# The first block's complex product in 45 frequency steps: two products summed on VectorE and one product of 512 columns back, in place of two products summed in PSUM

## The chip, the core and the metric

The kernel runs on one core of one Trainium2 chip. TensorE multiplies matrices into PSUM, VectorE (DVE), ScalarE (ACT) and GpSimd (POOL) work element by element, SyncE (SP) issues most DMAs. Each engine takes its own instructions strictly in the order of the program; semaphores hold an instruction back until what it needs is there. GpSimd has no access to PSUM. The metric is the device time of one execution in microseconds (us); lower is better.

## What is computed

The reference is a long convolution by FFT, followed by a gated mixture of experts. Only the convolution matters here:

```python
h_filt = (np.maximum(pos_emb @ w1, 0.0) @ w2) * window
u = x * v
L = 2 * S
Uf = np.fft.rfft(u, n=L, axis=1)
Hf = np.fft.rfft(h_filt, n=L, axis=0)
y = np.fft.irfft(Uf * Hf[None, :, :], n=L, axis=1)[:, :S, :]
return (x * y).astype(np.float32)
```

There are 4 sequences of 11456 positions and 128 channels, all in float32. The experts behind it are left out here; the change doesn't touch them.

## The kernel before

The sequence is cut into 3 blocks (NB) of 3840 positions, and the convolution is done by blocks: the spectrum of output block i is the sum over j of input block j times filter block i - j. So block 0 has one complex product, block 1 two, block 2 three. The channels are worked in 4 groups of 32 (NP, DH). A transform of 3840 is split into 60 x 64: a first transform of 60 (the first phase and the function data), one of 64 (spread), the product, one of 64 back, and one of 60 back in the last phase.

The frequency phase (freq_phase) goes through 60 steps: 4 channel groups of 15 steps, each for 4 of the 60 frequencies (KS), worked as two halves of 2 (KH). While it works on groups 0 to 2, it also carries the first transform of the following groups (others: GpSimd's product x * v at L185, the matmuls at L202, ScalarE's copies at L204); in the last 15 steps, the fourth group, it loads and prepares the experts in its place.

On the 128 partitions of a transform of 64, the real parts lie on partitions 0 to 63 and the imaginary parts on 64 to 127. One half step n, j goes like this:

- spread (L366 to L379): TensorE transforms signal and filter together, 480 columns a frequency, into the PSUM tile xp (L373). There is one xp for each half, xp0 and xp1, so the next step's spread waits until VectorE has read this step's. ScalarE then builds from the filter's spectrum the tile g, which holds for each block the filter and the same turned by 90 degrees (the halves of the partitions changed, one with its sign changed: L376, L377, L378).
- combine (L385, L386): VectorE makes the rest of g, from neighbouring filter blocks.
- mult (L393): VectorE multiplies the signal's blocks by g. The block-0 signal gives y (3 blocks x 2 factors, 1536 columns), the block-1 signal p1 (1024 columns), the block-2 signal p2 (512). The factor index a = 0, 1 is the plain and the turned filter: the two terms of a complex product are kept apart.
- After the second half GpSimd adds p1 and p2 into blocks 1 and 2 of y (L465, L466).
- back (L404), one step later (LAG = 1): for each block TensorE takes two products, one with each table c3[:, a], and sums them in PSUM. The tables transform back and form the complex product at once. ScalarE copies the result out (L405), and SyncE stores it.

The order in which a step is written is the order on every engine: half(0), combine(n, 1), back(0) of the step before, the spread of the next step's first half, the carried first transform (step: most times four matmuls of L202 and four copies of L204, in some steps eight, from step 42 on none), store, half(1), back(1), the next step's combine and second spread, GpSimd's sums, back(2). The results of back and of L202 share four PSUM buffers (the pool qps), so each of these products waits until the copy of the fourth one before it is done.

Of the kernel before, what the change touches and what calls it, by code (L numbers as in the profile page):

```python
# [10 lines left out]
F32 = mybir.dt.float32  # L11
# [3 lines left out]
AF = mybir.ActivationFunctionType  # L15
ALU = mybir.AluOpType
# [3 lines left out]
B, S, D = 4, 11456, 128  # L20
E, F = 8, 1024
NB = 3
# [6 lines left out]
DH = D // NP  # L29
# [48 lines left out]
def tables():  # L78

    k1 = np.arange(K1)  # L80
    k2 = np.arange(N2)
    n2 = np.arange(N2)
    n1 = np.arange(K1)
    th = 2 * np.pi * n1[:, None] * (k1[None, :] + 0.25) / K1
    c1 = np.zeros((2, 64, K1, 2))
    c1[:, :K1] = np.stack([np.cos(th), -np.sin(th)], axis=-1)
    ph = 2 * np.pi * n2[None, :, None] * (k1[:, None, None] + 0.25 + K1 * k2[None, None, :]) / L
    c2 = np.zeros((K1, 128, 128))
    c2[:, :64, :64] = np.cos(ph)
    c2[:, 64:, :64] = np.sin(ph)  # L90
    c2[:, :64, 64:] = -np.sin(ph)
    c2[:, 64:, 64:] = np.cos(ph)
    ps = 2 * np.pi * k2[:, None] * n2[None, :] / N2
    c3 = np.zeros((128, 2, 128))
    c3[:64, 0, :64] = np.cos(ps)
    c3[64:, 0, :64] = -np.sin(ps)
    c3[:64, 0, 64:] = np.sin(ps)
    c3[64:, 0, 64:] = np.cos(ps)

    c3 = np.stack([c3[:64, 0], -c3[:64, 0], c3[64:, 0], -c3[64:, 0]]).reshape(2, 128, 128).transpose(1, 0, 2)  # L100
    c3 = np.ascontiguousarray(c3.reshape(128, 2, 2, 64).transpose(0, 1, 3, 2)).reshape(128, 2, 128)
    al = 2 * np.pi * (k1[:, None, None] + 0.25) * (N2 * n1[None, None, :] + n2[None, :, None]) / L
    c4 = np.zeros((128, N2, 64))
    c4[:K1, :, :K1] = np.cos(al) / L
    c4[K1:2 * K1, :, :K1] = -np.sin(al) / L
    pos = np.arange(S, dtype=np.float32)
    win = np.zeros(NB * L, np.float32)
    win[:S] = np.exp(np.float32(-0.01) * pos)
    winp = np.zeros((2, 64, NB, H2), np.float32)
    winp[:, :60] = win.reshape(NB, 60, 2, H2).transpose(2, 1, 0, 3)  # L110
    row = np.arange(128)[:, None] * NS + np.arange(NS) + 1


    e = np.arange(E)
    mine = np.repeat(e, NS)[:, None]
    own, past = (mine == e).astype(float), (mine < e).astype(float)
    sums = np.concatenate([past, own, -(mine == e - 1).astype(float)], axis=1)
    col = np.arange(E * NS)

    shift = np.zeros((E, 2, E))  # L120
    shift[e, 0, e] = -1
    shift[e[1:], 0, e[:-1]] = 1
    shift[-1, 0, -1] = 0
    shift[:, 1] = e[:, None] <= e[None, :]
    bump = np.where(e < E - 1, CAP, 4 * CAP)
    runs = np.concatenate([np.tile(PL * np.arange(PQ), (E, 1)), np.where(e > 0, CAP, 0)[:, None]], axis=1)
    odd = own @ own.T * (col % NS == NS - 1)
    f = np.float32
    return {
        "c1": c1.reshape(128, 2 * K1).astype(f),  # L130
        "c2": np.ascontiguousarray(c2.reshape(K1 // KS, KS, 128, 128).transpose(0, 2, 1, 3)).reshape(K1 // KS, 128, -1).astype(f), "c3": c3.astype(f),
        "c4": np.ascontiguousarray(c4.reshape(128, 2, H2 // C4, C4, 64).transpose(2, 0, 3, 1, 4)).reshape(H2 // C4, 128, -1).astype(f),
        "win": winp.reshape(128, NB * H2), "val": row.astype(np.float16),
        "sums": sums.astype(np.float16), "runs": runs.astype(f), "lines": (PL * np.arange(PQ)).reshape(PQ, 1).astype(f),
        "grid": np.tile(np.arange(PQ + PL, dtype=np.float16) % PQ, (128, 1)),
        "rev": np.tile(np.arange(E, 0, -1, dtype=f), (128, 1)),
        "tri": (np.arange(128)[:, None] <= np.arange(128)[None, :]).astype(np.float16),
        "cols": (col[:, None] < col[None, :]).astype(np.float16), "odd": odd.astype(np.float16),
        "iota": np.tile(np.arange(NTAB, dtype=f), (E, 1)),
        "shift": shift.astype(np.float16), "bump": bump.reshape(E, 1).astype(f),  # L140
    }


class First:
# [6 lines left out]
    ALL = NP * STEPS  # L151
# [155 lines left out]
def freq_phase(tc, nc, i, fi, zd, c3, spare, loads):  # L307
# [6 lines left out]
    PER, KH = K1 // KS, KS // 2  # L314
    ALL = NP * PER
    HERE = spare.shape[1] // 128
    with (
# [48 lines left out]
        def spread(n, j):  # L366

            x1, g = xs[n], gs[n]  # L370
            xp = qpx.tile([128, KH, 512], F32, name=f"xp{j}")
            for k in range(KH):
                nc.tensor.matmul(xp[:, k, 0:(NS + NB) * DH], c2(n % PER * KS + j * KH + k), x1[:, j * KH + k], start=True, stop=True)  # L373
            t = xp[:, :, NS * DH:(NS + NB) * DH].rearrange("p k (s d) -> p k s d", d=DH)
            v = g[:, j].rearrange("p s a k d -> p a k s d")
            nc.scalar.copy(v[0:64, 1], t[64:128])  # L376
            nc.scalar.activation(v[64:128, 1], t[0:64], AF.Copy, scale=-1.0)  # L377
            nc.scalar.copy(v[:, 0, :, 0], t[:, :, 0])  # L378
            xps[n, j] = xp  # L379

        def combine(n, j):
# [3 lines left out]
            nc.vector.tensor_tensor(v[:, 0, :, 1:], t[:, :, 1:], v[:, 1, :, 0:NB - 1], ALU.subtract)  # L385
            nc.vector.tensor_tensor(v[:, 1, :, 1:], t[:, :, 0:NB - 1], v[:, 1, :, 1:], ALU.add)  # L386

        def mult(o, n, j, blk):

            m = 2 * (NB - blk)  # L390
            x = xps[n, j][:, :, blk * B * DH:(blk + 1) * B * DH].rearrange("p k (b d) -> p k b d", d=DH)
            v = gs[n][:, j, 0:NB - blk].rearrange("p s a k d -> p (s a) k d")
            nc.vector.tensor_tensor(o[:, :, :, j * KH:(j + 1) * KH].rearrange("p s a k b d -> p (s a) k b d"),  # L393
                                    x[:, None].broadcast_to([128, m, KH, B, DH]),
                                    v[:, :, :, None, :].broadcast_to([128, m, KH, B, DH]), ALU.mult)

        def backer(n, y):
            h, k = divmod(n, PER)
            z = qp.tile([128, KS, NS, DH], F32, name="z", bufs=4)

            def back(blk):
                zps = qps.tile([128, 512], F32, name="ps").rearrange("p (k b d) -> p k b d", k=KS, b=B)
                for a in range(2):
                    nc.tensor.matmul(zps, c3[:, a, :], y[:, blk, a], start=(a == 0), stop=(a == 1))  # L404
                nc.scalar.copy(z[:, :, blk * B:(blk + 1) * B], zps)  # L405
                if blk == NB - 1:
                    done_z.append((h, k, z))
            return back
# [12 lines left out]
        xs = {n: load(n) for n in range(QX - 1)}  # L421
        for _ in range(LEAD):
            next(todo)
        gs, xps = {}, {}

        def begin(n, j):
            if n < ALL:
                if j == 0:
                    gs[n] = qp.tile([128, 2, NB, 2, KH, DH], F32, name="g")
                spread(n, j)  # L430
        begin(0, 0)
        begin(0, 1)
        combine(0, 0)
        for n in range(ALL + LAG):
            back = backer(n - LAG, ys.pop(n - LAG)) if n >= LAG else lambda blk: None
            if n + QX - 1 < ALL:
                xs[n + QX - 1] = load(n + QX - 1)
            if n >= ALL - PER:
                next(loads, None)

            def half(j):
                mult(y, n, j, 0)
                mult(p1, n, j, 1)
                mult(p2, n, j, 2)
                del xps[n, j]
            if n < ALL:
                y = ys[n] = qp.tile([128, NB, 2, KS, B, DH], F32, name="y", bufs=3)
                p1 = qp.tile([128, NB - 1, 2, KS, B, DH], F32, name="p1")
                p2 = qp.tile([128, 1, 2, KS, B, DH], F32, name="p2")
                half(0)  # L450
                combine(n, 1)
            back(0)
            begin(n + 1, 0)
            step()
            store()
            if n < ALL:
                half(1)
                del gs[n], xs[n]
            back(1)
            if n + 1 < ALL:  # L460
                combine(n + 1, 0)
            begin(n + 1, 1)
            if n < ALL:
                if n < ALL - 1:
                    nc.gpsimd.tensor_tensor(y[:, 1:], y[:, 1:], p1, ALU.add)  # L465
                    nc.gpsimd.tensor_tensor(y[:, 2:], y[:, 2:], p2, ALU.add)  # L466
                else:
                    nc.gpsimd.tensor_tensor(y[:, 1], y[:, 1], p1[:, 0], ALU.add)
                    nc.vector.tensor_tensor(y[:, 2], y[:, 2], p1[:, 1], ALU.add)
                    nc.vector.tensor_tensor(y[:, 2], y[:, 2], p2[:, 0], ALU.add)  # L470
            back(2)
# [801 lines left out]
def program(tc, i, out):  # L1273
    nc = tc.nc
# [4 lines left out]
    with tc.tile_pool(name="mc", bufs=1) as mc:  # L1279
        wf = mc.tile([128, 2 * E * F], F32, name="wf")  # L1280
        fi = First(nc, i, x1d, x1f, mc, wf)
        spare = wf[:, fi.used:]
        c3 = mc.tile([128, 2, 128], F32, name="c3")
        first_phase(tc, fi)
        nc.scalar.dma_start(c3, i["c3"])
        nc.scalar.dma_start(zd.rearrange("p h r w -> (p h) r w")[:, H2 * 2 * K1:], i["none"])
# [73 lines left out]
```

## Time and profile before

| what | value |
|---|---|
| time, median of 3 runs | 1626.85 us (1624.58 to 1632.59) |
| the profiled execution's own time | 1626.78 us |
| its span, from first to last instruction | 1625.0 us |
| L404, the products back, on TensorE | 720 records of 597 ns, 331.3 us |
| L393, the complex products, on VectorE | 240 + 120 records, 217.4 + 210.8 us |
| L465, L466, GpSimd's sums | 59 of 4537 ns and 59 of 2356 ns |
| share of TensorE in the chain that ended last | 84% |

A float32 matmul shows as two records in the trace, each with a weight load (PEld) beside it, so the 360 products of L404 are 720 records. Rows of instructions in order of time give the start in us from the span's start, the length in us, engine, line, operation, output<-inputs, and the number of merged instructions; in brackets stands how long the engine was idle before, and what ended that. Rows of groups give the count, then busy time in us, mean length in ns, and the idle time before. Rows of stretches give the limits, the length, the busy time of PE, PEld, DVE, ACT and POOL each with its number of instructions, the granted TensorE clock, the busy share of the DMA engines and GB/s. A row of one line over the whole run gives the least, median and greatest length in ns. Ends of matmuls are modelled, and neighbouring rows of one engine can overlap.

### The profile page before, as it was taken

The numbers are of one execution on the slowest core, as the hardware profiler recorded it, in microseconds if no ns is written. First come the engines' busy times: TensorE is split into PE (matmuls) and PEld (weight loads), VectorE is DVE, ScalarE is ACT, GpSimd is POOL, SyncE is SP. The second block draws the span as 40 slices with busy tenths as digits, with TensorE's granted clock in tenths as the row PEclk, the third lists the DMA queues.
The fourth block names the chain that finished last, engine by engine and source line by source line (L and its number), as shares of the span: only waits on it lengthen the run. The fifth ranks groups of instructions, "written<-read, shape, count | busy, mean of one in ns | idle before, by whom it ended". The sixth has DMA issues, their size and how long they took to land.

```text
span 1625.0 us, 26505 instructions
## 1 busy us (share of the span) xinstructions
PE 1537.8 (95%) x8272; PEld 961.0 (59%) x8272; DVE 1203.4 (74%) x2424; ACT 794.3 (49%) x1677; POOL 1084.8 (67%) x850
## 2 busy tenths in 40 slices
PE   7985999999999999996789999999989999999997
PEld 2552444444444444442347766666767888888997
DVE  1324877888788799993877777777887777777886
ACT  4552455444544544442235544544345655556774
POOL 1112988888888878870156647855677888867885
PEclk9996999999999999997889999999999999999999
DMA  7998999999999799968978768877631111111110
GB/s 283 333 339 315 379 377 377 356 329 335 321 343 338 255 265 316 312 160 295 301 222 255 229 214 257 255 223 240 209 87 33 47 45 47 45 37 37 38 36 23
DMA packets 198532, 361.92 MB, mean 223 GB/s; under 512 B 64650, under 2 KB 138778, under 8 KB 198350
## 3 DMA queue, kind: packets, MB, share of 16 engines
q1 hardware_dynamic: 181078, 320.12, 58.9%
q0 software_dynamic: 16704, 38.89, 8.5%
q8 instruction: 67, 1.10, 0.3%
q10 hardware_dynamic: 608, 1.20, 0.2%
q14 instruction: 75, 0.61, 0.1%
HBM read 216.96 MB, written 145.69 MB: 223 GB/s over the span
## 4 chain that ended last, share of the span: by engine, by line
PE 84%; DMA 6%; DVE 5%; issue 3%; POOL 1%; ACT 1%; SPq 0%; DVEq 0%; ACTq 0%; POOLq 0%
PE ps L404 20%; PE xp L373 12%; PE bank L782 6%; PE y L1018 5%; PE ps L202 5%; PE my L834 4%; PE my L832 4%; PE hp L700 4%; PE my L833 4%; PE hp L702 4%; PE hp L701 4%; PE mh L700 2%; PE tp L1031 2%; PE mh L702 1%; PE mh L701 1%
## 5 line engine op out<-in xcount | busy, mean ns | idle before, releaser
L404 PE MATMUL ps<-y,c 128*128 128x512 f32 x720 | 331.3, 597 | 0.3
L465 POOL TENSOR_TENSOR y<-y,p 128x2048 f32<-128x2048 f32 x59 | 267.7, 4537 | 68.8 <-DVE p L393 68.8
L706 POOL DMA_INDIRECT out<-o,ids x186 | 199.9, 1075 | 123.3 <-DVE o L713 87.0
L404 PEld LDWEIGHTS ps<-y,c 128*128 128x128 f32 x720 | 133.4, 190 | 173.0 <-issue 155.9
L637 POOL DMA_INDIRECT xt<-out,ids x186 | 193.1, 1038 | 49.3 <-issue 30.6
L393 DVE TENSOR_TENSOR p<-xp,g 128x1024 f32<-128x1024 f32 x240 | 217.4, 947 | 0.0
L393 DVE TENSOR_TENSOR y<-xp,g 128x1536 f32<-128x1536 f32 x120 | 210.8, 1757 | 4.1
L821 DVE SCALAR_TENSOR_TENSOR hh<-hp,hh 128x1024 fp32r<-128x1024 f32 x130 | 158.4, 1219 | 68.3 <-ACT hh L820 68.1
L405 ACT COPY z<-ps 128x512 f32<-128x512 f32 x180 | 105.6, 586 | 176.5 <-PE ps L404 167.5
L820 ACT ACTIVATE hh<-hp 128x1024 fp32r<-128x1024 f32 x130 | 134.2, 1032 | 75.4 <-PE hp L702 75.4
L589 POOL DMA_INDIRECT lists<-pl,lies x32 | 53.6, 1676 | 141.0 <-DVE step L1116 72.3
L466 POOL TENSOR_TENSOR y<-y,p 128x1024 f32<-128x1024 f32 x59 | 139.0, 2356 | 4.6
L677 DVE TENSOR_TENSOR ws<-wf,ws 128x1024 fp32r<-128x1024 f32 x104 | 126.7, 1219 | 15.5 <-ACT ws L672 12.1
L610 POOL MEMSET idle<- 128x512 f16 x248 | 134.6, 543 | 0.2
L1018 PE MATMUL y<-zt,c 128*64 128x512 f32 x384 | 114.1, 653 | 19.8 <-DMA zt<-zd 11.2
L700 PE MATMUL hp<-hl,ws 128*128 128x512 f32 (+1 forms) x344 | 123.3, 359 | 3.5 <-DVE tb L626 1.9
L202 PE MATMUL ps<-wf,c 60*120 60x384 f32 x512 | 111.8, 532 | 14.8 <-DVE wf L185 14.3
L782 PEld LDWEIGHTS bank<-wd,h 128*128 128x128 f32 x896 | 104.2, 191 | 31.5 <-issue 31.4
L373 PE MATMUL xp<-x,wf 128*128 128x480 f32 x256 | 115.5, 575 | 7.3 <-issue 3.6
L204 ACT COPY wf<-ps 120x384 f32<-120x384 f32 x256 | 105.5, 493 | 29.5 <-PE ps L202 28.9
L702 PE MATMUL hp<-hl,ws 128*128 128x512 f32 (+1 forms) x344 | 116.4, 338 | 0.0
L834 PE MATMUL my<-hh,ws 128*128 128x512 f32 (+1 forms) x344 | 116.3, 338 | 0.0
(162 smaller groups left out, 3062.1 us busy)
## 6 DMA issues: line engine op xcount, KB each, us to landing
wf<-xv SPq DMA_DIRECT2D x64, 768.0 KB
zt<-zd SPq DMA_DIRECT2D x64, 768.0 KB
x1d<-wf SPq DMA_DIRECT2D x64, 720.0 KB
x<-x1d SPq DMA_DIRECT2D x60, 768.0 KB
zd<-z SPq DMA_DIRECT2D x118, 384.0 KB
out<-xm SPq DMA_DIRECT2D x96, 258.0 KB
ox<-xo SPq DMA_DIRECT2D x96, 256.0 KB
x1f<-fx POOLq DMA_DIRECT2D x16, 720.0 KB
```

Source lines behind the costliest of these rows:

```text
L202: nc.tensor.matmul(ps[p], self.c1[rows], u[rows, q * RUN:(q + 1) * RUN], start=True, stop=True)
L373: nc.tensor.matmul(xp[:, k, 0:(NS + NB) * DH], c2(n % PER * KS + j * KH + k), x1[:, j * KH + k], start=True, stop=True)
L393: nc.vector.tensor_tensor(o[:, :, :, j * KH:(j + 1) * KH].rearrange("p s a k b d -> p (s a) k b d"), x[:, None].broadcast_to([128, m, KH, ...
L404: nc.tensor.matmul(zps, c3[:, a, :], y[:, blk, a], start=(a == 0), stop=(a == 1))
L465: nc.gpsimd.tensor_tensor(y[:, 1:], y[:, 1:], p1, ALU.add)
L637: ins = nc.gpsimd.indirect_dma_start(out=xt[:, j], out_offset=None, in_=self.rows[0:have], in_offset=bass.IndirectOffsetOnAxis(ap=ids[:, j ...
L700: nc.tensor.matmul(hp, w[:, 0, c], hl[:, 0], start=True, stop=False)
L702: nc.tensor.matmul(hp, w[:, 1, c], hl[:, 0], start=False, stop=True)
L706: ins = nc.gpsimd.indirect_dma_start(out=self.rows, out_offset=bass.IndirectOffsetOnAxis(ap=ids[:, j:j + 1], axis=0), in_=o, in_offset=Non ...
L782: nc.tensor.matmul(bank[:, j * D:(j + 1) * D], h[f][:, j * 128:(j + 1) * 128], wd[s][:, f * D:(f + 1) * D], start=(f == 0), stop=(f == F / ...
L834: nc.tensor.matmul(y, w2[:, 1, c], h[:, 0], start=False, stop=(f == F // 128 - 1))
L1018: nc.tensor.matmul(y[p * 64:(p + 1) * 64], c4s[ch // C4][:, ch % C4, p, :], z[:, NP * p:NP * (p + 1)], start=True, stop=True)
```

## The change

In steps 0 to 44 (whole(n): all but the last channel group) block 0 is treated in another way. ScalarE makes, besides g, two more tiles for each half step: w, which holds the real part of the filter's first block on both halves of the partitions and then its imaginary part on both halves (four copies of 64 partitions x 64 columns), and turn, the block-0 signal turned by 90 degrees (two instructions of 64 partitions x 256 columns). The mult of the block-0 signal then leaves block 0 of the output out (low = 1: four factors in place of six). A new function, first, multiplies the signal by the one part of w and turn by the other, and sums the two products: three VectorE instructions of 256 columns, the last two with all their inputs in SBUF. The sum overwrites the first product in y. The way back of block 0 is then one product of 512 columns with a third table c3[:, 2], which transforms back and nothing else. Blocks 1 and 2, and all of the last 15 steps, are as before.

```diff
+    c3 = np.concatenate([c3, np.concatenate([c3[:64, 0], c3[:64, 1]])[:, None]], axis=1)
...
+            if whole(n):
+                turns[n, j] = qp.tile([128, KH, B * DH], F32, name=f"turn{j}", bufs=1)
             xp = qpx.tile([128, KH, 512], F32, name=f"xp{j}")
...
             nc.scalar.copy(v[:, 0, :, 0], t[:, :, 0])
+            if whole(n):
+                w, turned = ws[n][:, j], turns[n, j]
+                for half in range(2):
+                    here, there = slice(half * 64, half * 64 + 64), slice(64 - half * 64, 128 - half * 64)
+                    for a in range(2):
+                        nc.scalar.copy(w[here, a], t[a * 64:a * 64 + 64, :, 0])
+                    nc.scalar.activation(turned[here], xp[there, :, 0:B * DH], AF.Copy, scale=2.0 * half - 1.0)
             xps[n, j] = xp
...
-        def mult(o, n, j, blk):
-
-            m = 2 * (NB - blk)
+        def whole(n):
+            return n < ALL - PER
+
+        def first(y, n, j):
+
+            ks = slice(j * KH, (j + 1) * KH)
+            shape = [128, KH, B, DH]
+            x = xps[n, j][:, :, 0:B * DH].rearrange("p k (b d) -> p k b d", d=DH)
+            for a, v in enumerate((x, turns.pop((n, j)).rearrange("p k (b d) -> p k b d", d=DH))):
+                nc.vector.tensor_tensor(y[:, 0, a, ks], v, ws[n][:, j, a][:, :, None, :].broadcast_to(shape), ALU.mult)
+            nc.vector.tensor_tensor(y[:, 0, 0, ks], y[:, 0, 0, ks], y[:, 0, 1, ks], ALU.add)
+
+        def mult(o, n, j, blk, low=0):
+
+            m = 2 * (NB - blk - low)
...
-            v = gs[n][:, j, 0:NB - blk].rearrange("p s a k d -> p (s a) k d")
+            v = gs[n][:, j, low:NB - blk].rearrange("p s a k d -> p (s a) k d")
...
-                for a in range(2):
-                    nc.tensor.matmul(zps, c3[:, a, :], y[:, blk, a], start=(a == 0), stop=(a == 1))
+                if blk == 0 and whole(n):
+                    nc.tensor.matmul(zps, c3[:, 2, :], y[:, 0, 0], start=True, stop=True)
+                else:
+                    for a in range(2):
+                        nc.tensor.matmul(zps, c3[:, a, :], y[:, blk, a], start=(a == 0), stop=(a == 1))
...
             def half(j):
-                mult(y, n, j, 0)
+                mult(y[:, 1:] if whole(n) else y, n, j, 0, int(whole(n)))
                 mult(p1, n, j, 1)
                 mult(p2, n, j, 2)
+                if whole(n):
+                    first(y, n, j)
                 del xps[n, j]
...
-        c3 = mc.tile([128, 2, 128], F32, name="c3")
+        c3 = mc.tile([128, 3, 128], F32, name="c3")
```

How this stands on the engines is shown at two places of step 15. On VectorE, before, the second half of step 15 and the combine of the next step (xp is the half's PSUM tile, p the tiles p1 and p2; the numbers are those of the buffers):

```order
L393 TENSOR_TENSOR y<-xp_1849,g 128x6x256
L393 TENSOR_TENSOR p_1866<-xp_1849,g 128x4x256
L393 TENSOR_TENSOR p_1867<-xp_1849,g 128x2x256
L385 TENSOR_TENSOR g<-xp_1878,g 128x2x2x32
L386 TENSOR_TENSOR g<-xp_1878,g 128x2x2x32
```

The same place on VectorE in the changed kernel, whose lines are numbered anew (L415 is mult, L407 and L408 are first, L395 and L396 combine):

```order
L415 TENSOR_TENSOR y<-xp_2159,g 128x4x256
L415 TENSOR_TENSOR p_2182<-xp_2159,g 128x4x256
L415 TENSOR_TENSOR p_2183<-xp_2159,g 128x2x256
L407 TENSOR_TENSOR y<-xp_2159,w 128x256
L407 TENSOR_TENSOR y<-turn_2158,w 128x256
L408 TENSOR_TENSOR y<-y 128x256
L395 TENSOR_TENSOR g<-xp_2198,g 128x2x2x32
L396 TENSOR_TENSOR g<-xp_2198,g 128x2x2x32
```

The first mult has lost two of its six factors, and three instructions stand between the last mult and the next combine; two of them read no PSUM tile.

On ScalarE, before, from the spread of step 15's first half to that of its second (z is the output of back, wf the buffer of the carried transform):

```order
L376 COPY g<-xp_1817 64x2x3x32
L377 ACTIVATE g<-xp_1817 64x2x3x32
L378 COPY g<-xp_1817 128x64
L204 COPY wf<-ps 120x384 x4
L405 COPY z<-ps 128x4x128
L376 COPY g<-xp_1849 64x2x3x32
```

The same stretch of ScalarE in the changed kernel (L379 to L381 make g, L387 makes w, L388 makes turn, L205 is the copy of the carried transform, L430 that of z):

```order
L379 COPY g<-xp_2117 64x2x3x32
L380 ACTIVATE g<-xp_2117 64x2x3x32
L381 COPY g<-xp_2117 128x64
L387 COPY w<-xp_2117 64x64 x2
L388 ACTIVATE turn_2116<-xp_2117 64x256
L387 COPY w<-xp_2117 64x64 x2
L388 ACTIVATE turn_2116<-xp_2117 64x256
L205 COPY wf<-ps 120x384 x4
L430 COPY z<-ps 128x4x128
L379 COPY g<-xp_2159 64x2x3x32
```

Six instructions now stand between the copies that make g and those of the carried transform. GpSimd's instructions and their order are the same in both kernels.

More of the change, by code (lines that the diff above doesn't have):

```diff
@@ L423, in freq_phase @@
             next(todo)
-        gs, xps = {}, {}
+        gs, xps, ws, turns = {}, {}, {}, {}
         def begin(n, j):
@@ L429, in begin @@
                     gs[n] = qp.tile([128, 2, NB, 2, KH, DH], F32, name="g")
+                    if whole(n):
+                        ws[n] = qp.tile([128, 2, 2, KH, DH], F32, name="w")
                 spread(n, j)
@@ L441, in half @@
             def half(j):
-                mult(y, n, j, 0)
+                mult(y[:, 1:] if whole(n) else y, n, j, 0, int(whole(n)))
                 mult(p1, n, j, 1)
                 mult(p2, n, j, 2)
+                if whole(n):
+                    first(y, n, j)
                 del xps[n, j]
```

## The prediction

> **What bounds the kernel now.** I read the head of the page first, then two stretches of the trace, then single instructions in order of time.
>
> ```profile
> span 1625.0 us, 26505 instructions
> PE 1537.8 (95%) x8272; PEld 961.0 (59%) x8272; DVE 1203.4 (74%) x2424; ACT 794.3 (49%) x1677; POOL 1084.8 (67%) x850
> 148.00:600.00 452.00, 447.08 (x1242) 195.51 (x1242) 365.58 (x452) 222.24 (x580) 384.26 (x134) 1.00 0.96 337
> 294.90:305.00 10.10, 10.09 (x29) 4.38 (x28) 8.14 (x11) 5.00 (x13) 8.68 (x3) 1.00 1.04 371
> ```
>
> The profiled execution took 1626.78 us, 1.8 more than its span, and the median is 1626.85, so no correction is needed. The third row is the stretch of the first 45 steps, the fourth one step of it; after the length stand the busy times of PE, PEld, DVE, ACT and POOL, then the granted clock. In a step of 10.10 us TensorE is busy throughout, at full clock; GpSimd has 1.42 us free, VectorE 1.96 and ScalarE 5.10. A product taken from TensorE would pay at once, if nothing else grows past 10.10 us. The limits of the whole stretch are its two ends:
>
> ```profile
> 147.99 1.76 DVE L393 TENSOR_TENSOR y<-xp,g 128x1536 f32<-128x1536 f32 x1
> 600.32 1.74 DVE L393 TENSOR_TENSOR y<-xp,g 128x1536 f32<-128x1536 f32 x1
> ```
>
> VectorE begins step 0 at 147.99 and step 45 at 600.32: 45 steps in 452.3 us.
>
> **What is removed: TensorE.**
>
> ```profile
> 576.41 3.60 PE L404 MATMUL ps<-y,c 128*128 128x512 f32 x8
> 579.84 0.57 PE L373 MATMUL xp<-x,c 128*128 128x480 f32 x1
> ```
>
> Eight records of L404 take 579.84 - 576.41 = 3.43 us, 0.43 each, and one product is two records. Each of 45 steps loses one product, 0.86 us. If TensorE stayed the bound that would be 45 x 0.86 = 39 us.
>
> **What is added: VectorE's own time.** Per half step the block mult writes 1024 columns in place of 1536, and three instructions of 256 columns are new.
>
> ```profile
> 292.57 0.29 DVE L385 TENSOR_TENSOR g<-xp,g 128x128 f32<-128x128 f32 x1 [0.88 <-ACT g L378]
> 292.90 0.29 DVE L386 TENSOR_TENSOR g<-xp,g 128x128 f32<-128x128 f32 x1
> 293.23 1.76 DVE L393 TENSOR_TENSOR y<-xp,g 128x1536 f32<-128x1536 f32 x1
> 294.90 1.81 DVE L393 TENSOR_TENSOR p<-xp,g 128x1024 f32<-128x1024 f32 x2
> ...
> L393 DVE TENSOR_TENSOR p<-xp,g 128x1024 f32<-128x1024 f32 x90 | 109.3, 1214 | 0.0
> L393 DVE TENSOR_TENSOR p<-xp,g 128x512 f32<-128x512 f32 x90 | 61.3, 681 | 0.0
> ```
>
> I count from start to start, since neighbours overlap: 1.214 + 0.681 - 1.81 = 0.085 us. The two combines take 293.23 - 292.57 = 0.66. A mult of 1024 columns takes 1.214 - 0.085 = 1.13, one of 512 0.60. For 256 columns I go between 0.29 (128) and 0.681 (512): 0.42. The first new mult overlaps its successor (0.335); the second, and the sum, end before what follows may start (L385 to L386: 0.33 for 0.29), so 0.455 each. A half step is 0.66 + 1.13 + 1.13 + 0.60 + 0.335 + 0.455 + 0.455 = 4.77, a step 9.53 us. So without any wait VectorE would still be under 10.10.
>
> **What is added: VectorE and GpSimd collide.** This is the term that decides. Everything VectorE does now in these steps has one operand in PSUM (xp). The new second mult (turn times w) and the sum (y plus y) have both inputs in SBUF. Before has one place where VectorE does that while GpSimd adds:
>
> ```profile
> 724.25 2.35 POOL L468 TENSOR_TENSOR y<-y,p 128x1024 f32<-128x1024 f32 x1 [1.40 <-DVE p L393]
> ...
> 724.62 3.06 DVE L469 TENSOR_TENSOR y<-y,p 128x1024 f32<-128x1024 f32 x1
> 727.71 1.23 DVE L470 TENSOR_TENSOR y<-y,p 128x1024 f32<-128x1024 f32 x1
> ```
>
> L469 and L470 are the same sum. L470, with GpSimd idle, takes 1.23 us; L469, begun 0.37 after GpSimd's L468, takes 3.06 and ends 727.68 - 726.60 = 1.08 us after GpSimd does: it stood still until GpSimd had finished. GpSimd itself was not slowed (2.35 us here, 2.35 for L466 below). The counterweight is L677, also SBUF with SBUF, beside GpSimd's indirect DMAs and memsets:
>
> ```profile
> L677 DVE TENSOR_TENSOR ws<-wf,ws x104: 1202/1216/1227, 828.4 to 1610.3; 128x1024 fp32r<-128x1024 f32 x104
> ```
>
> None of 104 is stretched, so it takes a GpSimd instruction that reads SBUF as L468 does. In the Trainium skill, the page "SBUF — State Buffer", section "Who interferes with whom", states just this: a VectorE instruction with two SBUF inputs contends with a GpSimd instruction that reads SBUF, and whoever is second waits for the whole of the first. It speaks against this change. By it the two waits below are full ones; were the port shared in slices they would be near nothing. L469 shows a full wait, once.
>
> GpSimd's work in a step:
>
> ```profile
> 286.10 4.55 POOL L465 TENSOR_TENSOR y<-y,p 128x2048 f32<-128x2048 f32 x1 [1.36 <-DVE p L393]
> 290.72 2.35 POOL L466 TENSOR_TENSOR y<-y,p 128x1024 f32<-128x1024 f32 x1
> 293.03 1.82 POOL L185 TENSOR_TENSOR wf<-wf 124x768 f32<-124x768 f32 x1
> 296.19 4.54 POOL L465 TENSOR_TENSOR y<-y,p 128x2048 f32<-128x2048 f32 x1 [1.34 <-DVE p L393]
> ```
>
> L465 begins as soon as the second half's first p is written (294.90 + 1.214 = 296.11; L465 at 296.19). Put 0 at the end of that p. GpSimd holds 0.08 to 4.62. VectorE does the other p and the first new mult, and reaches the second at 1.13 + 0.60 + 0.335 - 1.214 = 0.85. As with L469 (1.08 after the release, 0.15 less than alone) it ends at 4.62 + 0.42 - 0.15 = 4.89 in place of 0.85 + 0.42 = 1.27: **3.62 us lost**. L466 follows L465 after 290.72 - 290.65 = 0.07 us, so it is waiting when that mult ends, while the sum can only start 0.03 later: L466 goes first, 4.89 + 2.35 = 7.24, and the sum ends 0.27 after, at 7.51, in place of 4.89 + 0.035 + 0.42 = 5.34: **2.17 us lost**. Then L185 runs to about 9.4. The first half of the next step comes to its second mult at 7.51 + 0.035 + 0.66 + 2.26 + 0.60 + 0.335 = 11.4, when GpSimd is idle, so it loses nothing. The step becomes 9.53 + 3.62 + 2.17 = **15.32 us**, VectorE the bound.
>
> The size of the second wait is unknown. At the low end the sum slips in ahead of L466 and loses nothing: 13.15 us. At the high end L185 too goes first, another 1.82: 17.14. I take the middle, since L466 is queued right behind L465 and VectorE's sum is not ready when the port comes free.
>
> **What is added: ScalarE.** Each half step gains four copies of 64 columns and two turns of 256.
>
> ```profile
> 296.76 0.32 ACT L376 COPY g<-xp 64x192 f32<-64x192 f32 x1 [1.07 <-DVE p L393]
> 297.08 0.32 ACT L377 ACTIVATE g<-xp 64x192 f32<-64x192 f32 x1
> 297.42 0.21 ACT L378 COPY g<-xp 128x64 f32<-128x64 f32 x1
> 297.54 1.63 ACT L204 COPY wf<-ps 120x384 f32<-120x384 f32 x4
> ...
> L405 ACT COPY z<-ps 128x512 f32<-128x512 f32 x130 | 76.2, 586 | 129.1 <-PE ps L404 121.2 <-DMA wf<-xv 6.8 <-DMA zd<-z 1.1
> L204 ACT COPY wf<-ps 120x384 f32<-120x384 f32 x180 | 72.8, 493 | 0.5 <-ACT g L378 0.5
> ```
>
> A copy of 64 columns is 0.21 us (L378). 256 columns lie between 192 (0.32) and 512 (0.586): 0.37. L376 and L377 are followed with no overlap, L378 is followed after 0.12. Wholly without overlap the six add 4 x 0.225 + 2 x 0.38 = 1.66, all overlapped like L378 4 x 0.12 + 2 x 0.28 = 1.04. I take 1.56: five of the six change the half of the partitions that they read or write, as L376 and L377 do. ScalarE goes from 5.00 to 8.1 us a step; with a step of 15.32 that is covered, and the turned values are ready long before VectorE asks for them. Only the first step pays openly, two half steps of copies before VectorE begins: 3 us.
>
> If the cover were gone, it would cost in one place. Four L204 free the PSUM buffers for which the next L404 waits:
>
> ```profile
> 296.61 1.55 PE L202 MATMUL ps<-wf,c 60*120 60x384 f32 x8
> 298.17 1.95 PE L404 MATMUL ps<-y,c 128*128 128x512 f32 x4
> ```
>
> The first L204 ends at 297.54 + 0.49 = 298.03, and L404 starts at 298.17, right after it: TensorE and ScalarE are even here today. So 1.56 us more ahead of L204 moves this product by 1.56, against 0.86 saved: +0.70 a step. The extra c3 columns and SBUF tiles move no transfer that the steps wait for.
>
> **The sum.** 45 x 15.32 = 689.4; less 452.3 = 237; with the 3 us at the start 1626.8 + 240 = **1867 us**. Behind step 45 the work is as before and moves as a whole. With the ends of the second wait: 45 x 13.15 gives 1769, 45 x 17.14 gives 1949.
>
> **The rivals.**
> First, no wait between VectorE and GpSimd for such short instructions. For it: L677 never waits, and a 256-column read needs the port for a quarter of a microsecond. Against it: L469. Then ScalarE's copies decide, 45 x 0.70 = 32 and 3 at the start: 1661 us.
> Second, on the other side, **the product saved is really saved**: no port wait, and the new copies overlap or are hidden so that the L404 behind the four L204 is moved by clearly less than 0.86 us. Then TensorE stays the bound and gets 39 us back: 1588. Against it: even the cheapest sum, 1.04, is over 0.86, and TensorE has no slack at that point. If the two about cancel there is no change, within 0.5% or 8 us, about what a measurement of this kernel can tell.
> Third, TensorE loses its clock. In the forecast it works 10.10 - 0.86 = 9.24 us of 15.32 and idles 6 a step, and this trace has a half clock behind shorter gaps:
>
> ```profile
> 793.71 0.16 PE L548 MATMUL bank<-tnt,shift 8*8 8x1 f16 x1 [1.93 <-DVE tnt L542]
> ...
> 795.00:799.00 4.00, 4.00 (x24) 1.74 (x22) 3.63 (x14) 1.04 (x3) 0.00 (x0) 0.57 0.66 179
> ```
>
> A 1.93 us gap, then 0.57 of the clock. The 9.24 us at half clock are 18.5, more than 15.32; held there all the time it would bound the step: 45 x 18.5 gives about 2010. But a busy TensorE has the full clock in this trace, so at most a part of each step is slow, and 6 us of slack cover that.
> In the Trainium skill, "TensorE: Matmul & The Clock Gate", Part 1, puts the idle time that halves the clock at about 3.4 us; this trace has it behind 1.93 us, so the row counts.
>
> **Chances and range.** Forecast with its two ends 0.82, no wait 0.07, lost clock 0.04, real saving 0.04, no change 0.03. So slower 0.93, same 0.03, faster 0.04. The range is the forecast's own, 1769 to 1949, a little widened: 1760 to 1950.
>
> **What would show it.** The new second mult (L407 of the changed kernel, from turn) would have two durations, 0.42 in the first half and about 4 us in the second; the sum (L408) 0.42 and about 2.6. GpSimd's adds stay 4.54 and 2.35. TensorE's busy share in this stretch falls to about 60%, the step is 15.3 us, and the chain of waits runs over VectorE. If L407 and L408 stay near 0.4 us throughout, the port term is wrong, and a step of 10.8 us with TensorE waiting for the copy behind ScalarE's turns would be the first rival. A step of 9.2 to 9.5 us would be the second.

## The result, and the profile after

The changed kernel takes 1853.82 us (median of six runs, 1851.22 to 1855.28) against 1629.45 us for the kernel before (six runs, 1624.58 to 1639.52): a ratio of 1.1358, interval 1.1335 to 1.1381. The forecast was 1867 us.

First the head of the page of the changed kernel, with its row of the granted clock, then the stretch of the first 45 steps and one step in it (columns as in the prediction: length, busy time of PE, PEld, DVE, ACT, POOL, granted clock).

```profile
span 1853.5 us, 27220 instructions
PE 1574.3 (85%) x8182; PEld 956.1 (52%) x8182; DVE 1500.3 (81%) x2694; ACT 920.9 (50%) x2217; POOL 1101.1 (59%) x850
PEclk9977998999999998889989799999999999999999
```

```profile
150.16:822.41 672.25, 484.51 (x1162) 192.35 (x1162) 662.35 (x723) 348.28 (x1117) 399.63 (x137) 0.91 0.74 230
382.56:397.48 14.92, 10.75 (x34) 4.30 (x32) 14.71 (x17) 9.33 (x33) 8.89 (x4) 1.00 0.70 196
```

VectorE is busy 14.71 of 14.92 us in a step, where it had been busy 8.14 of 10.10; TensorE, busy for 10.09 of 10.10 before, now stands still for 4.2. The stretch from VectorE's step 0 to its step 45 has grown from 452.3 to 672.25 us, by 219.9. That leaves 8.6 of the 228.5 us between the two spans: 2.2 at the start (150.16 against 147.99) and 6.4 behind step 45 (1853.5 - 822.41 = 1031.1 against 1024.7), no more than runs of one kernel differ by.

Where the VectorE time sits shows in the same page's groups (busy us, mean ns of one), and in the durations of single source lines (least/median/greatest ns). All 90 instances of a line have one shape, so a mean hides nothing but time:

```profile
L407 DVE TENSOR_TENSOR y<-turn,w 128x256 f32<-128x256 f32 x90 | 198.4, 2204 | 0.0
L408 DVE TENSOR_TENSOR y<-y 128x256 f32<-128x256 f32 x90 | 131.0, 1456 | 3.1
```

```profile
L407 DVE TENSOR_TENSOR y<-xp,w x90: 412/415/416, 153.0 to 814.6; 128x256 f32<-128x256 f32 x90
L407 DVE TENSOR_TENSOR y<-turn,w x90: 415/2288/4098, 153.4 to 815.0; 128x256 f32<-128x256 f32 x90
L408 DVE TENSOR_TENSOR y<-y x90: 424/2177/2466, 155.3 to 819.1; 128x256 f32<-128x256 f32 x90
```

The first mult, which reads xp in PSUM, takes 0.41 us every time. The second, of the same size but from turn in SBUF, goes from 0.415 to 4.1 us, and the sum from 0.42 to 2.47. The timeline of VectorE and of GpSimd over the second half of one step and the first half of the next (start, duration) shows beside what they stretch:

```profile
396.18 1.81 DVE L415 TENSOR_TENSOR p<-xp,g 128x1024 f32<-128x1024 f32 x2
397.91 0.41 DVE L407 TENSOR_TENSOR y<-xp,w 128x256 f32<-128x256 f32 x1
398.24 4.04 DVE L407 TENSOR_TENSOR y<-turn,w 128x256 f32<-128x256 f32 x1
402.31 2.45 DVE L408 TENSOR_TENSOR y<-y 128x256 f32<-128x256 f32 x1
404.69 0.28 DVE L395 TENSOR_TENSOR g<-xp,g 128x128 f32<-128x128 f32 x1
...
408.53 0.41 DVE L407 TENSOR_TENSOR y<-turn,w 128x256 f32<-128x256 f32 x1
408.98 0.43 DVE L408 TENSOR_TENSOR y<-y 128x256 f32<-128x256 f32 x1
```

```profile
397.48 4.52 POOL L494 TENSOR_TENSOR y<-y,p 128x2048 f32<-128x2048 f32 x1 [5.96 <-DVE p L415]
402.07 2.40 POOL L495 TENSOR_TENSOR y<-y,p 128x1024 f32<-128x1024 f32 x1
404.44 1.99 POOL L186 TENSOR_TENSOR wf<-wf 124x768 f32<-124x768 f32 x1
```

GpSimd's first sum ends at 402.00, VectorE's second mult at 402.28; GpSimd's second sum ends at 404.47, VectorE's sum at 404.76. In the first half, at 408.53, GpSimd is idle and the same two instructions take 0.41 and 0.43. The chain of waits, by engine and then by line, ends the reading:

```profile
PE 50%; DVE 32%; issue 9%; DMA 5%; ACT 2%; POOL 0%; SPq 0%; DVEq 0%; ACTq 0%; POOLq 0%
DVE y L407 11%; DVE p L415 8%; DVE y L415 5%; PE ps L429 5%; PE bank L811 4%; PE y L1047 4%; PE xp L376 4%; PE hp L729 3%; PE hp L731 3%; PE my L863 3%; PE my L861 3%; PE my L862 3%; PE hp L730 3%; PE mh L729 2%; PE tp L1060 2%
```

L407 leads it. GpSimd has 0%, although the experiments below show that it is what L407 waits for: L407 has no idle time and no releaser, so the page books the wait as VectorE's own work. Only the spread of durations gives it away. In what follows "the port" stands for whatever the two engines share here; the runs show when one of them waits, not the port itself.

### The profile page after: what moved, and what is told of

It reads as the page before. It is cut to its first block, busy times and chain, and to the rows that moved or that the text cites. A ratio compares the mean times of both kernels' runs of the same rounds, so it can differ in the third digit from the quotient of the medians.

```text
span 1853.5 us, 27220 instructions
## 1 busy us (share of the span) xinstructions
PE 1574.3 (85%) x8182; PEld 956.1 (52%) x8182; DVE 1500.3 (81%) x2694; ACT 920.9 (50%) x2217; POOL 1101.1 (59%) x850
## 4 chain that ended last, share of the span: by engine, by line
PE 50%; DVE 32%; issue 9%; DMA 5%; ACT 2%; POOL 0%; SPq 0%; DVEq 0%; ACTq 0%; POOLq 0%
DVE y L407 11%; DVE p L415 8%; DVE y L415 5%; PE ps L429 5%; PE bank L811 4%; PE y L1047 4%; PE xp L376 4%; PE hp L729 3%; PE hp L731 3%; PE my L863 3%; PE my L861 3%; PE my L862 3%; PE hp L730 3%; PE mh L729 2%; PE tp L1060 2%
## 5 line engine op out<-in xcount | busy, mean ns | idle before, releaser
L429 PE MATMUL ps<-y,c 128*128 128x512 f32 x540 | 255.3, 601 | 43.0 <-ACT wf L205 43.0
L735 POOL DMA_INDIRECT out<-o,ids x186 | 201.6, 1084 | 122.3 <-DVE o L742 86.0
L415 DVE TENSOR_TENSOR p<-xp,g 128x1024 f32<-128x1024 f32 x240 | 217.4, 948 | 0.0
L407 DVE TENSOR_TENSOR y<-turn,w 128x256 f32<-128x256 f32 x90 | 198.4, 2204 | 0.0
L376 PE MATMUL xp<-x,wf 128*128 128x480 f32 x256 | 138.7, 673 | 70.1 <-issue 64.3
L429 PEld LDWEIGHTS ps<-y,c 128*128 128x128 f32 x540 | 100.3, 192 | 177.8 <-issue 171.2
L379 ACT COPY g<-xp 64x192 f32<-64x192 f32 x120 | 37.9, 316 | 282.3 <-PE xp L376 282.2
L415 DVE TENSOR_TENSOR y<-xp,g 128x1024 f32<-128x1024 f32 (+1 forms) x120 | 162.8, 1357 | 4.1
L430 ACT COPY z<-ps 128x512 f32<-128x512 f32 x180 | 103.5, 587 | 117.2 <-PE ps L429 87.1
L376 PE MATMUL xp<-x,c 128*128 128x480 f32 x224 | 118.7, 659 | 47.9 <-issue 46.3
L203 PE MATMUL ps<-wf,c 60*120 60x384 f32 x512 | 125.8, 592 | 18.1 <-DVE wf L186 15.2
L706 DVE TENSOR_TENSOR ws<-wf,ws 128x1024 fp32r<-128x1024 f32 x104 | 127.2, 1223 | 14.0 <-ACT ws L701 10.8
L408 DVE TENSOR_TENSOR y<-y 128x256 f32<-128x256 f32 x90 | 131.0, 1456 | 3.1
L729 PE MATMUL hp<-hl,ws 128*128 128x512 f32 (+1 forms) x344 | 123.5, 359 | 4.5 <-DVE hh L850 2.1
```

The lines of the kernel that those rows point to most:

```text
L407: nc.vector.tensor_tensor(y[:, 0, a, ks], v, ws[n][:, j, a][:, :, None, :].broadcast_to(shape), ALU.mult)
L729: nc.tensor.matmul(hp, w[:, 0, c], hl[:, 0], start=True, stop=False)
L735: ins = nc.gpsimd.indirect_dma_start(out=self.rows, out_offset=bass.IndirectOffsetOnAxis(ap=ids[:, j:j + 1], axis=0), in_=o, in_offset=Non ...
```

## The experiments

Three explanations of the 220 us were set against each other: the port (theory A: VectorE's instructions with two SBUF inputs wait for GpSimd's), ScalarE's six copies in front of L205 (theory B), and new VectorE instructions that are simply slow (theory C). All runs are compared by the stretch from VectorE's step 0 to step 45 (452.3 us before, 672.3 after) as well as by the whole time. A stretch is that of the one profiled execution, and a step is counted from the start of VectorE's first mult to that of the next step's.

**GpSimd's two sums left out in the 45 steps.**

```
@@ the end of the second half step
+                if whole(n):
+                    pass
-                if n < ALL - 1:
+                elif n < ALL - 1:
                     nc.gpsimd.tensor_tensor(...)
```

> The changed kernel without GpSimd's two sums in steps 0 to 44 (blocks 1 and 2 of these steps lack what p1 and p2 bring). Theory A (port: VectorE's instructions with two SBUF inputs stand until GpSimd's sum has ended, 3.6 + 2.0 us a step): the second mult and the sum both take 0.42 us in all 90 half steps, and what limits next is ScalarE's six copies ahead of the carried transform's copies: step 10.8 us, 1661 us (1645 to 1670). Theory B (the new ScalarE copies hold up VectorE): unchanged, step 14.9 us, about 1850. Theory C (these SBUF instructions are slow by themselves): unchanged, about 1850, the second mult still 2.2 us in the mean.

Measured: 1666.4 us, ratio 1.0229 (1.017 to 1.0288); stretch 488.0, a steady step 10.67. Of the 220 us, 184 go with the two sums. The time is the expected one, but the second mult is not at 0.42 us in every half step. The timeline of VectorE in this kernel has the pair of one half step at its own speed, and the mult of the next half step still stretched; GpSimd's timeline names the instruction beside it.

```profile
403.67 0.41 DVE L407 TENSOR_TENSOR y<-turn,w 128x256 f32<-128x256 f32 x1
404.11 0.42 DVE L408 TENSOR_TENSOR y<-y 128x256 f32<-128x256 f32 x1
...
408.40 1.71 DVE L407 TENSOR_TENSOR y<-turn,w 128x256 f32<-128x256 f32 x1
```

```profile
408.03 1.81 POOL L186 TENSOR_TENSOR wf<-wf 124x768 f32<-124x768 f32 x1 [8.87 <-PE ps L203]
```

The instructions aren't slow by themselves. And GpSimd's third SBUF reader, the carried product L186, now falls on VectorE's second mult: it ends at 409.84, the mult at 410.11. In the same step TensorE stands still for 1.41 us until the first L205, behind ScalarE's new copies, is done (TensorE's timeline):

```profile
409.26 1.98 PE L429 MATMUL ps<-y,c 128*128 128x512 f32 x4 [1.41 <-ACT wf L205]
```

**ScalarE's new copies left out after step 0.** The w and turn tiles of step 0 stay in use, and the copies run under `if n == 0`.

> The changed kernel with w and turn made by ScalarE in step 0 alone and read again in all later steps (block 0 is wrong there). Theory A: ScalarE's copies were hidden behind VectorE's waits, so the time stays within 8 us of the changed kernel's 1854 (step 14.9 us). Theory B: the step falls to the 9.5 us of VectorE or the 9.3 us of TensorE, below 1630. Theory C: unchanged, 1854.

Measured: 1874.36 us, ratio 1.1506 (1.1439 to 1.1573); stretch 671.2, step 14.91. The stretch is that of the changed kernel, 672.3: the copies cost nothing while the port is the bound. The whole time is 20 us longer, outside the expected 8. Of these, 18 lie behind step 45 (1049.6 against 1031.1 us), probably because the experts' work there depends on the computed values (the trace has 188 indirect DMAs of line L735 in place of 186); from here on, kernels that compute other values are read by their stretch.

**Both left out.**

> Both left out: no GpSimd sums in steps 0 to 44, and w and turn made in step 0 alone. Theory A: only VectorE's own instructions are left as a bound, 9.53 us a step, 45 x 9.53 = 429 in place of 452: about 1604 us (1595 to 1615), faster than before the change. Theory C: over 1800. Theory B: as its run without copies.

Measured: 1630.64 us, ratio 1.0018 (0.9994 to 1.0042); stretch 447.8. The expectation, 1595 to 1615, was missed. The step is 9.27 us in most of steps 1 to 12 and 10.00 in most from step 14 to 38, where VectorE's timeline shows both instructions stretched again, by L186:

```profile
404.82 1.15 DVE L407 TENSOR_TENSOR y<-turn,w 128x256 f32<-128x256 f32 x1
406.01 1.91 DVE L408 TENSOR_TENSOR y<-y 128x256 f32<-128x256 f32 x1
```

```profile
403.88 3.76 POOL L186 TENSOR_TENSOR wf<-wf 124x768 f32<-124x768 f32 x2 [8.19 <-PE ps L203]
```

Two L186 fill 403.88 to 407.64; the mult ends at 405.97, between them, and the sum at 407.92, after the second. Leaving out two of GpSimd's three readers does not free the port. The 9.27 us of the early steps are VectorE's own time: there L407 and L408 take 0.41 and 0.42 us.

**The sums left out and the copies moved behind L205.** The w and turn copies go into a function of their own, called after the step's L205.

```
+        def extra(n, j):
...
             step()
+            extra(n + 1, 0)
```

> As the run without GpSimd's sums, but ScalarE makes w and turn behind the carried transform's copies and not ahead of them. If it is their place ahead of these copies that makes a step of 10.8 us (TensorE waits for a PSUM buffer), the step falls to 9.5 to 10.1 us, 1605 to 1630. If it is ScalarE's or VectorE's amount of work, it stays as in the run without sums, about 1661.

Measured: 1639.92 us, ratio 1.0056 (1.0036 to 1.0076); stretch 460.0, step 10.11, at the upper end of what was expected; the time is 10 us above it. Against the first experiment (10.67) only ScalarE's order differs, and it is worth 0.56 us a step: a cost that does not show while GpSimd's sums are there. VectorE's second mult still waits for L186, for 0.85 us a step where it was 1.30 in the first experiment, so part of the 0.56 can lie there; the two were not separated.

**The suspected cost by itself, in the kernel before.** One added VectorE instruction of 256 columns per step behind the second half's last p, its result unused: once with both inputs in SBUF, once with one of them in PSUM.

```
+ nc.vector.tensor_tensor(probe, y[:, 0, 0, ks], y[:, 0, 1, ks], ALU.add)      # first kernel
+ nc.vector.tensor_tensor(probe, <xp, block 0>, y[:, 0, 1, ks], ALU.add)       # second kernel
```

> The kernel before, with one VectorE instruction more in steps 0 to 44: behind the second half's last mult a sum of 256 columns with both inputs in SBUF, into a tile that nobody reads. Nothing else of the change. Theory A: it comes 0.5 us after GpSimd has begun its 4.54 us sum and ends with it, some 4.4 us long; VectorE's step becomes 8.12 + 0.42 + 3.95 = 12.5 us, 45 x 12.5 = 562 in place of 452: about 1737 us (1720 to 1750). Without a port wait (or with GpSimd slowed instead) it takes 0.42 us, hidden in VectorE's 1.96 us of slack: 1627.

> The same as the run before it, but one of the two inputs of the added sum is in PSUM (the signal's block 0 in xp). Theory A: no port is shared, 0.42 us, hidden in the slack: within 8 us of 1627. If any instruction more at this place costs, whatever it reads (VectorE is the hidden bound there): the same as the run before it.

Measured: 1718.31 us, ratio 1.0528 (1.0498 to 1.0559), stretch 536.9, step 12.37; and 1633.57 us, ratio 1.0025 (1.0003 to 1.0047), stretch 454.0, step 10.10. The second is as expected. The first is 2 us below its range of 1720 to 1750: the step is nearly the expected one, but in nine of the 45 the probe takes only 0.42 to 1.7 us. The two timelines, first the kernel with SBUF and SBUF, VectorE and GpSimd, then the other:

```profile
402.97 4.36 DVE L448 TENSOR_TENSOR probe<-y 128x256 f32<-128x256 f32 x1
```

```profile
402.53 4.51 POOL L469 TENSOR_TENSOR y<-y,p 128x2048 f32<-128x2048 f32 x1 [3.58 <-DVE p L393]
```

```profile
407.02 0.42 DVE L448 TENSOR_TENSOR probe<-xp,y 128x256 f32<-128x256 f32 x1
```

```profile
406.58 4.54 POOL L469 TENSOR_TENSOR y<-y,p 128x2048 f32<-128x2048 f32 x1 [1.34 <-DVE p L393]
```

Same place, same size, both 0.44 us behind the start of GpSimd's sum: 4.36 us against 0.42. One operand in PSUM is all the difference, and it is 85 us of the stretch against 2. Both read the tile y that GpSimd is adding to, so it is not the tile that one waits for.

**GpSimd kept as busy, but only writing.** Three memsets of 2048 columns (5.53 us) stand in place of the two sums.

```
+                if whole(n):
+                    for _ in range(3):
+                        nc.gpsimd.memset(p1, 0.0)
```

> The changed kernel with GpSimd's two sums of steps 0 to 44 replaced by three memsets of p1, which write SBUF and read nothing (blocks 1 and 2 of these steps lack p1 and p2). If the wait comes from GpSimd reading SBUF: the second mult and the sum stay at 0.42 us beside the memsets, step 10.7 us as in the run without sums, 1666 us give or take 25 for the experts' other work with other data. If any GpSimd instruction at work holds VectorE up: the second mult is as long as what is left of the memset beside it, 1 us or more.

Measured: 1666.95 us, in a single run, and within the expected range; stretch 484.0, step 10.77. VectorE and GpSimd in this kernel:

```profile
402.61 0.41 DVE L407 TENSOR_TENSOR y<-turn,w 128x256 f32<-128x256 f32 x1
403.06 0.42 DVE L408 TENSOR_TENSOR y<-y 128x256 f32<-128x256 f32 x1
...
407.69 1.92 DVE L408 TENSOR_TENSOR y<-y 128x256 f32<-128x256 f32 x1
```

```profile
401.82 5.53 POOL L495 MEMSET p<- 128x2048 f32 x3 [3.26 <-DVE p L415]
407.32 2.02 POOL L186 TENSOR_TENSOR wf<-wf 124x768 f32<-124x768 f32 x1
```

In the midst of the memsets nothing waits; beside L186, which reads SBUF, the sum does. A busy GpSimd is not the condition, a reading one is.

**The same work, asked for earlier.** The plain mult goes right behind the first block mult of its half, and the second half issues both second mults and both sums ahead of its p, that is before GpSimd's sums can start.

```
                 if whole(n):
+                    plain(y, n, j)
+                    if j == 1:
+                        first(y, n, 0)
+                        first(y, n, 1)
                 mult(p1, n, j, 1)
```

> The changed kernel computing the same, with the SBUF instructions of both halves (second mult and sum) moved: they stand in the second half ahead of the p1 mult whose end starts GpSimd's 4.54 us sum, at the end of GpSimd's round. Theory A: they meet the tail of GpSimd's work (the end of the 2.35 us sum and the carried product of 1.82 us) in place of the 4.54 us sum, some 1.9 us lost in place of 5.6: step 11.3 to 11.5 us, about 1690 (1660 to 1710). Theory C, or a cost by number of instructions: unchanged, 1854.

Measured: 1715.5 us, ratio 1.0511 (1.0464 to 1.0558); stretch 533.8. The order alone, with the same instructions, gives back 138 of the 220 us. Time and step stay above what was expected: steps of 11.51 and 12.11 alternate. VectorE's timeline over such a pair:

```profile
399.12 1.18 DVE L412 TENSOR_TENSOR y<-turn,w 128x256 f32<-128x256 f32 x1
...
409.88 0.29 DVE L395 TENSOR_TENSOR g<-xp,g 128x128 f32<-128x128 f32 x1 [2.75 <-ACT turn L388]
```

In one step the mult meets L186 (398.20 to 400.01 on GpSimd), in the other VectorE stands 2.75 us waiting for ScalarE's turn. Followed back in the trace, this is the same collision again: the mult stretched by L186 holds the one buffer of turn, ScalarE's next turn waits 0.35 us for it, L205 stands behind that turn, TensorE waits 1.95 us for L205, and the spread that the late turn reads comes after that.

**A version meant to win.** The second mult can be kept off the port, and the sums made one: the imaginary w is copied into 32 spare columns of xp in PSUM, so that the mult has a PSUM operand, and one sum of 512 columns replaces two of 256. It runs one step later, placed where GpSimd should be between its second sum and L186; ScalarE's copies stand behind its first two L205, and the way back of block 0 behind that of block 2.

```
-                        nc.scalar.copy(w[here, a], t[a * 64:a * 64 + 64, :, 0])
+                    nc.scalar.copy(w[here], t[0:64, :, 0])
+                    nc.scalar.copy(xp[here, :, (NS + NB) * DH:], t[64:128, :, 0])
...
+        def total(n):
+                nc.vector.tensor_tensor(ys[n][:, 0, 0], ys[n][:, 0, 0], ys[n][:, 0, 1], ALU.add)
```

> A version that computes the same as the changed kernel with the port in mind: the imaginary part of w lies in the free columns of xp in PSUM, so the second mult reads only one input from SBUF; the sum of both halves is one instruction of 512 columns, one step later, placed so that it meets the change from GpSimd's 2.35 us sum to its carried product; ScalarE's new copies stand behind the first two copies of the carried transform, and back(0) behind back(2). Theory A: one port user meets GpSimd, at most 0.5 us lost, step 9.4 to 10.0 us in place of 10.05 before: about 1605 us (1595 to 1627), at or below the kernel before. If VectorE's new instructions are costly for another reason than the port: above 1650.

Measured: 1639.26 us, ratio 1.0056 (1.0036 to 1.0075); stretch 457.8; most steps 9.54 to 9.61, eight of the 45 some 10.7, and the four that carry two L186 12.6 to 14.5. The time lies above the expected 1595 to 1627 and below the 1650 of the other case. The timelines of VectorE and GpSimd show what the steps of 9.54 and of 10.7 differ in:

```profile
304.40 2.33 DVE L420 TENSOR_TENSOR y<-y 128x512 f32<-128x512 f32 x1
...
413.08 0.70 DVE L420 TENSOR_TENSOR y<-y 128x512 f32<-128x512 f32 x1
```

```profile
304.37 1.82 POOL L186 TENSOR_TENSOR wf<-wf 124x768 f32<-124x768 f32 x1
...
413.19 4.04 POOL L186 TENSOR_TENSOR wf<-wf 124x768 f32<-124x768 f32 x2
```

At 304.37 L186 is 0.03 us ahead and the sum waits it out; such a sum, of 2.31 to 2.34 us, stands in each of the eight. At 413.08 the sum is first; of the two L186 behind it, 4.04 us in all where two take 3.64, one now does the waiting.

To let the sum go first always, GpSimd got a short memset between its second sum and L186, of 256 and of 512 columns:

> The version with the port in mind, and a GpSimd memset of 256 columns (0.23 us at the rate of the memset run) between its second sum and the carried product, in steps 0 to 44. In the version without it most steps took 9.54 us, but about every third 10.8, where VectorE's sum came 0.03 us after the carried product had begun and stood for its 1.8 us. Theory A: the sum slips in beside the memset, which reads nothing; all steps take 9.5 to 9.6 us, some 12 steps x 1.27 = 15 us less than 1639: 1620 to 1628, at or just below the kernel before. If the long steps have another cause (transfers, GpSimd's load): 1635 to 1645, as without it.

> The same with a memset of 512 columns (0.46 us). Theory A: as with 256 columns, or up to 5 us more if GpSimd's round (4.54 + 2.37 + 0.46 + 1.82 to 2.28) then reaches the step's length: 1620 to 1633. If the long steps have another cause: 1635 or more.

Measured: 1631.77 us, ratio 1.0009 (0.9989 to 1.0029), stretch 448.1; and 1630.12 us, ratio 0.9992 (0.998 to 1.0004), stretch 446.6. The first is above its expected range of 1620 to 1628, which had counted some 12 long steps where there are eight; the second is within. The waits of the sum are gone and the steps take 9.54, except for the first two, those with two L186, which take 12.6 to 14.4, and the last three. In a step with two L186 TensorE waits for GpSimd's second L186 (kernel with 256 columns, TensorE's timeline, then GpSimd over 100 us in the row of a stretch, 97.09 busy):

```profile
409.21 2.30 PE L203 MATMUL ps<-wf,c 60*120 60x384 f32 x8 [1.35 <-POOL wf L186]
```

```profile
300.00:400.00 100.00, 99.29 (x276) 40.99 (x275) 94.01 (x157) 81.60 (x263) 97.09 (x44) 1.00 0.99 352
```

In the stretch 4 to 6 us are gained on the kernel before, and in the whole time no difference can be told. The row has TensorE busy for 99.29 of 100 us and GpSimd for 97.09: both are full now. In the kernel with 256 columns the steps of 9.54 save some 19 us against the same steps before, and 15 of these are lost again: the first two steps take 23.1 us in place of 16.2, the four with two L186 52.7 in place of 48.1, the last three 28.7 in place of 25.4. No version here beat the kernel before.

## Why the prediction was right

The term that it called decisive was right in mechanism, place and nearly in size.

- **TensorE's product** is gone as said. It was worth nothing, since VectorE became the bound.
- **VectorE's own time.** Forecast 9.53 us a step, shown 9.27 by the early steps of the kernel without sums and copies. Most of the difference is the sum's overlap with its successor, which was put at nothing: L408 of 402.31 ends at 404.76, and L395 starts at 404.69, 0.07 before. Over 45 steps 12 us.
- **The port: first wait.** Forecast 3.62; 4.04 - 0.415 = 3.62. The mult ends 0.28 us behind GpSimd's sum, 0.27 was forecast.
- **The port: second wait.** Forecast 2.17, measured 2.45 - 0.425 = 2.02. GpSimd's second sum did go first, as the middle of the range had it.
- **Together** 9.27 + 3.62 + 2.02 = 14.91, the steady step is 14.92, the forecast 15.32: 45 x 0.40 = 18 us too many, of which 6 are made up behind step 45; the rest is the difference of some 12 us between 1867 and the profiled execution.
- **The rule of the Trainium skill** (page "SBUF — State Buffer", section "Who interferes with whom") is that a VectorE instruction with two SBUF inputs contends with a GpSimd instruction that reads SBUF, and not with one that only writes it. The runs here agree on each point: two SBUF inputs on VectorE (4.36 us) and not one (0.42), a GpSimd instruction that reads (1.92 beside L186) and not one that writes (0.41 beside memsets). What VectorE waits out is the whole rest of the other instruction (its mult ends 0.28 us behind GpSimd's sum). GpSimd's side is not quite as still as the forecast had it: its sums keep 4.52 and 2.40, but L186, behind VectorE's sum, takes 1.99 for 1.82.
- **ScalarE's copies** were forecast as hidden, and as 0.70 us a step if they were not (the first rival, 10.8 us a step, 1661 us). Without the copies the stretch is unchanged (671.2); without the sums the kernel takes 10.67 a step and 1666 us. That agrees in size, and TensorE waits where the rival put it: 1.41 us for L205, where 1.56 was forecast. Moving the copies takes 10.67 - 10.11 = 0.56 off, part of which can be L186 on the port, as said above. The six copies of a half step take 1.55 us in that run (402.99 to 404.54) where 1.56 was forecast, although only four of them change the half of the partitions, not five as the prediction says.
- **The clock.** The third rival's lower clock did come, in part: 0.91 in the stretch, 1.00 in the step shown. TensorE's busy share is 484.51 / 672.25 = 72%, not the 60% named as a marker. Slower matmuls are part of that; records that end later behind a gap may be the rest, which wasn't tried. The slack covered it, as forecast: VectorE has 0.2 us left of 14.92, TensorE 4.2.
- **The real saving** (second rival, 1588 us) had one more bar in its way than was named. By an estimate the port alone has to carry GpSimd's reading, 4.54 + 2.35 + 1.82 = 8.71 us, and four VectorE instructions of 0.42, together 10.4 us, more than the 10.10 of the step before. If these exclude each other for their whole lengths, no order of this change's instructions can win; but an instruction that has waited ends 0.28 us after its release, and by that the total is 8.71 + 4 x 0.28 = 9.8, so this is not shown. With one sum of 0.70 the total is 9.4, and the steps did run at 9.54.

What the experiments got wrong had mostly one cause: with GpSimd's sums gone or dodged, L186 was counted as harmless, because in the changed kernel it comes behind VectorE's pair (404.44, just before the sum's end). In these kernels it meets them (both left out: 1631 where 1604 was expected; earlier order: 1715 for 1690).

## What to carry to other kernels

As far as this kernel shows: before work moves to VectorE, list its instructions that would have both inputs in SBUF and GpSimd's that read SBUF, and add their times up as if one engine ran them; if the sum is over the step, put one operand into PSUM or leave the work where it is. The length of the waiting instruction says nothing of its price (0.42 us of work, 4 us of time), while who asks first does: the price is what is left of the other instruction. In a trace look for one shape with two durations, since such a wait has no releaser and counts as busy.

## What was not expected of the hardware

The engine that comes second by 0.03 us (the sum of 512 columns at 304.40) waits the other's instruction out to its end, and here the port changed hands only between instructions: VectorE's mult ended 0.28 us after GpSimd's sum, and GpSimd's next sum, started 0.07 after the first, held back VectorE's next instruction, due 0.03 after its mult (402.31), for the whole of its 2.40 us. So a VectorE pair can lose to a GpSimd pair twice in a row, 3.62 + 2.02 us, though VectorE needs the port for less than 1. A GpSimd instruction that starts beside VectorE's waits as well, but visibly less here: L186 takes 1.99 us beside a sum's tail in place of 1.82, and 4.04 for two in place of 3.64 behind a sum of 512 columns.
